# An RWKV attention and two-MLP kernel on one core: the second group's k products in split operands, and later preparation for the last five units

## The chip, the cores and the metric

The kernel runs on one core of a Trainium2 chip. The metric is the device time of one execution in microseconds; the number given for a kernel is the median of several runs. TensorE is called PE here, VectorE DVE, ScalarE ACT, GpSimd POOL and SyncE SP, as in the profile; SP and ACT also issue DMAs.

## What is computed

Three layers in float32, over 2 batches of 768 tokens.

```python
# attention: 8 heads of 48; state is 48 x 48 per head
for t in range(S):
    cur = einsum('bhd,bhe->bhde', u[None] * kt, vt)
    y[:, :, t] = einsum('bhd,bhde->bhe', rt, state + cur)
    state = wt[:, :, :, None] * state + einsum('bhd,bhe->bhde', kt, vt)
# first MLP, x is the attention's output, 384 wide
xk = mu_k * x + (1.0 - mu_k) * x_prev        # x_prev: the token before
xr = mu_r * x + (1.0 - mu_r) * x_prev
k = np.maximum(xk @ w_k, 0.0)                # 384 -> 1024
x = 1 / (1 + exp(-(xr @ w_r))) * (k * k @ w_v)
# second MLP, with a mixing over tokens
h = gelu(x @ w_in); u, v = halves of h
out = x + (u * (w_sg @ norm(v) + b_sg)) @ w_out
```

## The kernel before

Tokens are worked in four groups of 384 (0 to 3). In a group attention has four **units**, one per pair of heads, so units 0 to 15; unit i belongs to group i // 4. A unit is chunked in three parts of 128 tokens. Its work on PE is four steps: S(i) (`attn_sc`: transposes of kp, the sums `ab` of the direct term, and the scores `sc`), K(i) (`attn_kv`: the state products `kv`), Y(i) (`attn_y`: the masked scores `am` times v), Z(i) (`attn_z`: the carried states, then the output `yo`, which a DMA puts into the group's x, `xx`).

Before S(i), `attn_prep` makes on DVE the decay scans `pf` and `pr`, and the operands `kp`, `rp` and `ru`. `scans` runs it up to the two scans and issues the next unit's loads; `products` runs the rest; `prep` runs all. After S(i), DVE takes `ru<-ab` and the two mask products `am` (L482); after K(i) it makes the states `zt` and `zcar` (L508, L510), which ACT scales into `sblk` and `scar` (L524) for Z.

The first MLP of a group has three stages on PE: eight k steps (`moe1_k`, three 128-row products each over the blocks of x), three r steps (`moe1_r`), and v steps (`moe1_v`, 24 products of each output block). The matmul helper is `mm` (L595, matmuls at L603). While a group's MLP runs, the next group's units are put between its steps: the list `plan` at the start of `emit` says after which k, r and v step which S, K, Y and Z comes, with estimated durations from which `TS` and `TE` (times of start and end) are made. PE follows that list by hand. On the other engines a scheduler orders the instructions by the priority that `at(t)` gives them; `tc.issue_after(x)` keeps an instruction from being placed before x on its engine. Each engine then works its queue strictly in order, and waits at its head.

Products have two forms. **Natural**: both operands float32, one matmul instruction per product, which the trace shows as two records. **Split**: each operand is a rounded high part and the rest, and a product is three matmuls (high x high, high x low, low x high). For split products ACT makes the high part by a copy and the low part is a subtraction (`split_to`, L311): of the weights on POOL, of x on DVE (L642, L643). `NAT` says how many groups use the natural form of k, r and v: groups 0 and 1 for k, group 0 for r and v.

`moe1_prep(s, which)` makes the operand of group s, k (0) or r (1), block by block: ACT scales x by mu (`dx`, L637), DVE adds the scaled token before (L639), and if split, ACT copies the high part and DVE subtracts. Block 2 of group 1 needs unit 7's output. `split1` splits a weight of the first MLP; its low part goes to the next free tile of a ring of 21 that the full weights use too. In group 1, a k step's `split1` made one low part of k on POOL. The r and v weights are split at the end of group 0's v stage (L711). `load64` loads and converts a weight (`top` on ACT, then L309 on DVE); the w_in weights of the second MLP (`wf`) take tiles of the same ring.

Of the kernel before, what the change touches and what calls it, by code (L numbers as in the profile page):

```python
# [24 lines left out]
NP = H // 2  # L25
# [19 lines left out]
B_AM = 2  # L45
B_KP = 3
T_START = 7
T_GAP = 2.5
T_TAIL = 9.0
VQ = 4  # L50
# [4 lines left out]
L_CK = 6  # L55
L_PREP = 5
L_UN = 14
NAT = {"k":2,"r":1,"v":1}
SUB0 = (3,)
NVN = 8  # L60
RA = 12
# [8 lines left out]
def emit(tc, tin, nin, vt, consts, ucp, pars, b_sg, w_k, w_v, w_r, w_in, w_sgT, w_out, outT):  # L70
# [239 lines left out]

    def split_to(hi, lo, full, dl, e):  # L311
        with at(dl):
            A.activation(hi, full, AF.Copy)  # L313
            e.tensor_tensor(lo, full, hi.bitcast(F32), ALU.subtract)  # L314

    def full1(nm, i, shape):
        wt[nm, i] = (pl["w"].tile(shape, F32, name="w" + nm, tag="wl", bufs=NW1 + SPARE),)

    def split1(nm, i, dl):
        if not split_ops[0]:  # L320
            return
        full = wt[nm, i][0]
        shape = list(full.shape)
        lo = pl["w"].tile(shape, F32R, name="w" + nm + "l", tag="wl", bufs=NW1 + SPARE)
        if early["hi"] % 2 == 0:
            early["t"] = pair()
        o = early["hi"] % 2 * WT
        early["hi"] += 1
        hi = early["t"][:, o:o + WT].rearrange("p (c f) -> p c f", c=shape[1])
        split_to(hi, lo, full, dl, PL)  # L330
        wt[nm, i] = (hi, lo)

    def conv_moe1(first=0, last=2 * KF + KM):
        def one(nm, i, src, dl):
# [141 lines left out]
    def self_am(i, am, sc, tY):  # L476
        s = st[i]
        nc_ = subs[i // NP][2]
        for h in range(2):
            with at((TS["K", i] - 1.4 if i >= NP else tY - 1.2) + 0.4 * h):  # L480
                mask = cmask[:, None, :].to_broadcast([128, nc_, CH])
                V.tensor_tensor(am[:, h], sc[h], mask, ALU.mult)  # L482
        s["at"] = am

    def attn_kv(i):
        tY = TS["Y", i] if i < NP else TS["K", i] + 1.1
        s = st[i]
        hp = i % NP
        g, c0, nc_ = subs[i // NP]
        si = i // NP  # L490
        last = g % GB == GB - 1 and c0 + nc_ == CG
        nk = nc_ - 1 if last else nc_
        kv = pq.tile([128, 512], F32, name="kv", tag="kv", bufs=1)
        kv3 = kv[0:PR, 0:nc_ * D].rearrange("p (c d) -> p c d", d=D)
        for c in range(nk):
            for h in range(2):
                hs = slice(h * HP, HP if h == 0 else PR)
                PE.matmul(kv3[hs, c], s["kt"][:, c, hs], uv[i][:, c, h * D:h * D + D], start=(c == 0), stop=(c == nk - 1),  # L498
                          skip_group_check=True)
        zt = pa.tile([PR, max(1, nc_), D], F32, name="zt", tag="zt", bufs=2)  # L500
        first = g % GB == 0 and c0 == 0
        us = [None if first else scar[hp]]
        z = None if first else (zcar[:, (si + 1) % 2, hp, 0:D], zcar[:, (si + 1) % 2, hp, D:D + 1])
        for c in range(nk):
            o = zcar[:, si % 2, hp, 0:D] if c == nc_ - 1 else zt[:, c]
            with at(tY - 0.6 + (3 if c == nc_ - 1 else 0.2 * c)):
                if z is None:
                    V.tensor_copy(o, kv3[:, c])  # L508
                else:
                    V.scalar_tensor_tensor(o, z[0], z[1], kv3[:, c], ALU.mult, ALU.add)  # L510
            z = (o, s["pe"][c])
            sb = scar[hp] if c == nc_ - 1 else sblk[i % 2][c]

            def scaled(c=c, o=o, sb=sb):
                if c == nc_ - 1:
                    with at(tY + 3):
                        A.activation(zcar[:, si % 2, hp, D:D + 1], s["pe"][c], AF.Copy)
                with at(tY - 0.5 + (3 if c == nc_ - 1 else 0.2 * c)):
                    for h in range(2):
                        hs = slice(h * HP, h * HP + D)  # L520
                        if i == NP - 1 and c < nc_ - 1:
                            V.tensor_scalar(sb[hs, hs], o[hs], s["pe"][c][hs], None, ALU.mult)
                        else:
                            A.activation(sb[hs, hs], o[hs], AF.Copy, scale=s["pe"][c][hs])  # L524

            if i < NP:
                s.setdefault("late" if c == nc_ - 1 else "soon", []).append(scaled)
            else:
                scaled()
            us.append(sb)  # L530
        s["us"] = us
# [131 lines left out]
    def moe1_k(s, f):  # L663
        nat, nt = is_nat(s, "k"), subs[s][2] * CH
        ps = mm_tile()[:, 0:nt]
        mm(ps, [(part(wt["k", f], slice(None), j), part(m1[s, 0], slice(None), j)) for j in range(KM)])
        kr = pl["w"].tile([128, nt], F32, name="kr", tag="kr", bufs=2)
        te, tv = TE["k", s, f], TS["v", s, 0] + f * MM[s, "v"]
        with at(te):
            m1[s, "ev", f] = A.activation(kr, ps, AF.Relu).ins  # L670
        vn = is_nat(s, "v") and (f < NVN or not split_ops[0])
        kh = pl["w"].tile([128, nt], F32 if vn else F32R, name="kh", tag="kh", bufs=KF)
        dl = min(te + 1, tv - 2)
        if s == NAT["k"] - 1:
            split1("k", f, TS["k", s + 1, f])
        if vn:
            with at(dl):
                A.activation(kh, kr, AF.Square)
            m1[s, "k", f] = (kh,)
            return  # L680
        if f % 2 == 0:
            m1[s, "kl"] = klpair(F32R)
        kl = m1[s, "kl"][:, f % 2 * WT:f % 2 * WT + nt]
        with at(dl):
            A.activation(kh, kr, AF.Square)
            A.activation(kr, kr, AF.Square)  # L686
            V.tensor_tensor(kl, kr, kh.bitcast(F32), ALU.subtract)  # L687
        m1[s, "k", f] = (kh, kl)
# [10 lines left out]
    def moe1_v(s, j, q):  # L699
# [9 lines left out]
        with at(TE["v", s, j] - 0.5):  # L709
            V.tensor_tensor(x2[g][:, j, c0 * CH:(c0 + n) * CH], ps, m1[s, "r", j], ALU.mult)  # L710
        if s == NAT["r"] - 1 and j == KM - 1 and split_ops[0]:  # L711
            with tc.issue_after(st[2 * NP - 2]["ev"]):
                for f in range(KM):
                    split1("r", f, TS["r", s + 1, f])
                for f in range(NVN):
                    split1("v", f, TS["v", s + 1, 0] + f * 0.49)
# [223 lines left out]
                pass  # L940

    def scans(i):
        if i >= 1:
            load_unit(i + 1)
        head["prep", i] = attn_prep(i)
        next(head["prep", i])
        next(head["prep", i])

    def products(i):
        for _ in head["prep", i]:  # L950
            pass
# [14 lines left out]
    for n, key in enumerate(keys[:n_in]):  # L966
# [38 lines left out]
        if kd == "S" and g == NP:  # L1005
            prep(NP + 1)
            conv_moe1(3)
        if kd == "Z" and g >= NP:
            prep(g + 2)
            if g % NP == NP - 1:  # L1010
                moe1_prep(g // NP, 0)
        if kd == "k" and key[2] == (0 if g in (0, NS - 1) else KM - 1):
            moe1_prep(g, 1, [] if g in (0, NS - 1) else [m1[g, "ev", f] for f in range(KM)])
        if key == ("r", 0, 0):
            with at(TS["S", 2 * NP] - 20):
# [89 lines left out]
```

## Time and profile before

| | us |
|---|---|
| median of 3 runs (348.79 to 349.15) | 349.04 |
| the profiled execution | 351.7 |
| its span, first to last instruction | 349.8 |
| PE busy in it | 337.5 |
| DVE, ACT, POOL busy in it | 237.6, 180.9, 40.8 |
| mean granted PE clock, share of full speed | 0.994 |

Stages in the span: attention of group 0 until about 31, group 0's MLP with units 4 to 7 until 87.6, group 1's MLP with units 8 to 11 until 142.7, groups 2 and 3 until about 217, then the second MLP. A row gives start and duration in us; "x12" counts records; in brackets stands how long the engine was idle before the row and what released it. Matmuls overlap, so the spacing of starts tells what one costs, and its own duration does not. For the other engines too the spacing of starts is a little shorter than the duration of one.

### The profile page before, as it was taken

The numbers are of one execution on the slowest core, as the hardware profiler recorded it, in microseconds if no ns is written. First come the engines' busy times: TensorE is split into PE (matmuls) and PEld (weight loads), VectorE is DVE, ScalarE is ACT, GpSimd is POOL, SyncE is SP. The second block draws the span as 40 slices with busy tenths as digits, with TensorE's granted clock in tenths as the row PEclk, the third lists the DMA queues.
The fourth block names the chain that finished last, engine by engine and source line by source line (L and its number), as shares of the span: only waits on it lengthen the run. The fifth ranks groups of instructions, "written<-read, shape, count | busy, mean of one in ns | idle before, by whom it ended". The sixth has DMA issues, their size and how long they took to land.

```text
span 349.8 us, 5957 instructions
## 1 busy us (share of the span) xinstructions
PE 337.5 (96%) x2155; PEld 287.6 (82%) x2155; DVE 237.6 (68%) x520; ACT 180.9 (52%) x427; POOL 40.8 (12%) x64
## 2 busy tenths in 40 slices
PE   7999999999979989999999999999999999999993
PEld 3776677666546769988899999899899999999993
DVE  6987999794468886496438753298789951645531
ACT  3465986475665652686428894668171316211100
POOL 3000000064622000000004044000000000000000
PEclk9999999999989999999999999999999999999999
DMA  8787963762304541001113232822322010100022
GB/s 227 196 301 233 321 166 90 200 162 56 133 18 103 143 133 36 4 16 42 37 27 132 80 105 69 254 53 62 79 63 57 0 46 24 44 25 0 0 72 75
DMA packets 23750, 33.97 MB, mean 97 GB/s; under 512 B 3504, under 2 KB 18032, under 8 KB 23712
## 3 DMA queue, kind: packets, MB, share of 16 engines
q1 hardware_dynamic: 21568, 31.09, 30.7%
q10 hardware_dynamic: 2144, 2.41, 2.4%
q8 instruction: 19, 0.31, 0.4%
q14 instruction: 19, 0.16, 0.1%
HBM read 28.77 MB, written 2.36 MB: 89 GB/s over the span
## 4 chain that ended last, share of the span: by engine, by line
PE 64%; ACT 4%; DVE 4%; DMA 2%; issue 1%; SPq 1%; ACTq 0%; DVEq 0%
PE mm L603 31%; PE mn L603 27%; PE y L542 2%; DMA stg<-w_in 1%; PE sc L459 1%; PE y L556 1%; ACT wh L313 1%; PE ab L455 1%; ACT sblk L524 1%; DVE dx L639 1%; DMA xx<-yo 1%; DVE kl L687 1%; PE kv L498 1%; ACT dx L637 0%; ACT kr L670 0%
## 5 line engine op out<-in xcount | busy, mean ns | idle before, releaser
L603 PE MATMUL mm<-xkh,wk 128*128 128x384 f32 x96 | 35.6, 515 | 0.0
L591 ACT ACTIVATE gah<-gt 128x384 fp32r<-128x384 f32 x16 | 8.4, 526 | 43.3 <-DVE gt L783 43.3
L603 PEld LDWEIGHTS mm<-xkh,wk 128*128 128x128 f32 x96 | 18.2, 198 | 12.9 <-issue 2.3
L637 ACT ACTIVATE dx<-xx,par 128x384 f32<-128x384 f32 x22 | 13.3, 610 | 26.9 <-DMA xx<-yo 25.8
L524 ACT ACTIVATE sblk<-zt,pf 48x48 f32<-48x48 f32 x60 | 19.8, 331 | 11.0 <-DVE zt L508 7.1
L603 PE MATMUL mm<-kh,wh 128*128 128x384 f32 x64 | 22.1, 345 | 0.0
L603 PE MATMUL mm<-kh,wvl 128*128 128x384 f32 x64 | 21.6, 338 | 0.0
L603 PE MATMUL mm<-kl,wh 128*128 128x384 f32 x64 | 21.6, 337 | 0.0
L687 DVE TENSOR_TENSOR kl<-kr,kh 128x384 fp32r<-128x384 f32 x24 | 14.3, 594 | 10.5 <-ACT kr L686 10.5
L314 POOL TENSOR_TENSOR w2l<-wf,w2h 128x384 fp32r<-128x384 f32 x12 | 12.9, 1090 | 62.9 <-ACT w2h L313 62.9
L603 PE MATMUL mn<-wsh,vh 128*128 128x384 f32 x60 | 20.0, 334 | 0.0
L603 PE MATMUL mn<-wsl,vh 128*128 128x384 f32 x60 | 20.0, 334 | 0.0
L603 PE MATMUL mn<-wsh,vl 128*128 128x384 f32 x60 | 20.0, 334 | 0.0
L414 DVE TENSOR_TENSOR_SCAN pf<-uw,d1f 112x387 f32<-112x387 f32 x16 | 15.3, 959 | 4.8 <-DMA uw<-tin 2.2
L639 DVE SCALAR_TENSOR_TENSOR dx<-xx,par,dx 128x384 f32<-128x384 f32 x15 | 12.1, 809 | 9.6 <-ACT dx L637 9.6
L670 ACT ACTIVATE kr<-mm 128x384 f32<-128x384 f32 x27 | 12.9, 478 | 10.8 <-PE mm L603 8.9
L542 PE MATMUL y<-am,uv 128*48 128x128 f32 (+1 forms) x192 | 15.3, 278 | 2.4 <-DVE am L482 2.4
L482 DVE TENSOR_TENSOR am<-sc,cst 128x384 f32<-128x384 f32 x32 | 16.1, 545 | 1.1 <-PE sc L459 1.1
L603 PE MATMUL mm<-kh,wv 128*128 128x384 f32 x48 | 16.3, 490 | 0.0
L459 PEld LDWEIGHTS sc<-rp,kp 48*128 48x128 f32 x192 | 12.0, 187 | 5.1 <-issue 4.5
L419 DVE TENSOR_TENSOR_SCAN pr<-uw,d1r 112x387 f32<-112x387 f32 x16 | 15.4, 962 | 0.4
L459 PE MATMUL sc<-rp,kp 48*128 48x128 f32 x192 | 15.0, 289 | 0.0
(215 smaller groups left out, 965.3 us busy)
## 6 DMA issues: line engine op xcount, KB each, us to landing
urk<-tin SPq DMA_DIRECT2D x26, 144.0 KB, 3.5
wh<-w_k SPq DMA_DIRECT2D x8, 384.0 KB, 3.8
stg<-w_in SPq DMA_DIRECT2D x8, 384.0 KB, 3.6
wq<-tin SPq DMA_DIRECT2D x16, 168.0 KB, 2.4
wsf<-w_sgT SPq DMA_DIRECT2D x12, 192.0 KB, 4.0
outT<-ot SPq DMA_DIRECT2D x12, 192.0 KB, 1.9
uv<-nin ACTq DMA_DIRECT2D x14, 144.0 KB, 2.9
uw<-tin SPq DMA_DIRECT2D x26, 72.8 KB, 3.3
```

What stands on the lines that cost most here:

```text
L314: e.tensor_tensor(lo, full, hi.bitcast(F32), ALU.subtract)
L414: V.tensor_tensor_scan(pf[:, 0:n1], w[:, 0:n1], d1f[:, 0:n1], 1.0, ALU.mult, ALU.max)
L419: V.tensor_tensor_scan(pr[:, 1:wl][:, ::-1], w[:, 1:wl][:, ::-1], dr[:, 1:wl][:, ::-1], 0.0, ALU.mult, ALU.add)
L459: PE.matmul(sc[h][:, c], s["kp"][hs, c], s["rp"][hs, c], start=True, stop=True)
L482: V.tensor_tensor(am[:, h], sc[h], mask, ALU.mult)
L524: A.activation(sb[hs, hs], o[hs], AF.Copy, scale=s["pe"][c][hs])
L542: PE.matmul(y3[hs, c], uv[i][:, c, h * D:PW if h else HP], s["at"][:, h, c], start=(c == 0), stop=False, skip_group_check=True)
L603: PE.matmul(ps, l, r, start=(first and k == 0), stop=(last and k == len(prods) - 1))
L637: A.activation(d, xj[:, 1 + t0:1 + t1], AF.Copy, scale=mu[:, j:j + 1])
L639: V.scalar_tensor_tensor(ops[0][:, j] if nat else d, xj[:, t0:t1], nu[:, j:j + 1], d, ALU.mult, ALU.add)
L670: m1[s, "ev", f] = A.activation(kr, ps, AF.Relu).ins
L687: V.tensor_tensor(kl, kr, kh.bitcast(F32), ALU.subtract)
```

## The change

- `NAT["k"]` goes from 2 to 1: group 1's k steps use split operands too, so 24 natural products become 72 split matmuls, and blocks of group 1's x for k get a high and a low part.
- The eight k weights are split at the end of group 0's v stage, right after unit 7's output eviction in the order, ACT for the high part and DVE (was POOL) for the low part. The r and v weights follow behind the last k copy on ACT; before they followed unit 6's eviction.
- Group 1's r operand is prepared right behind its k operand (`moe1_prep(1, 1)` after Z(7)), not spread over the first k steps.
- Units 11 to 15: the scans are held behind the states of the unit two before, and kp, rp, ru behind the mask products of the unit just before. Before they were placed by priority alone.

```diff
@@ -45,6 +45,7 @@
 B_AM = 2
 B_KP = 3
 T_START = 7
+UPIN = 11
 T_GAP = 2.5
 T_TAIL = 9.0
 VQ = 4
@@ -55,7 +56,7 @@
 L_CK = 6
 L_PREP = 5
 L_UN = 14
-NAT = {"k":2,"r":1,"v":1}
+NAT = {"k":1,"r":1,"v":1}
 SUB0 = (3,)
 NVN = 8
 RA = 12
@@ -310,13 +311,14 @@
 
     def split_to(hi, lo, full, dl, e):
         with at(dl):
-            A.activation(hi, full, AF.Copy)
+            i = A.activation(hi, full, AF.Copy).ins
             e.tensor_tensor(lo, full, hi.bitcast(F32), ALU.subtract)
+        return i
 
     def full1(nm, i, shape):
         wt[nm, i] = (pl["w"].tile(shape, F32, name="w" + nm, tag="wl", bufs=NW1 + SPARE),)
 
-    def split1(nm, i, dl):
+    def split1(nm, i, dl, e=PL):
         if not split_ops[0]:
             return
         full = wt[nm, i][0]
@@ -327,8 +329,9 @@
         o = early["hi"] % 2 * WT
         early["hi"] += 1
         hi = early["t"][:, o:o + WT].rearrange("p (c f) -> p c f", c=shape[1])
-        split_to(hi, lo, full, dl, PL)
+        ins = split_to(hi, lo, full, dl, e)
         wt[nm, i] = (hi, lo)
+        return ins
 
     def conv_moe1(first=0, last=2 * KF + KM):
         def one(nm, i, src, dl):
@@ -479,7 +482,7 @@
         for h in range(2):
             with at((TS["K", i] - 1.4 if i >= NP else tY - 1.2) + 0.4 * h):
                 mask = cmask[:, None, :].to_broadcast([128, nc_, CH])
-                V.tensor_tensor(am[:, h], sc[h], mask, ALU.mult)
+                s["am"] = V.tensor_tensor(am[:, h], sc[h], mask, ALU.mult).ins
         s["at"] = am
 
     def attn_kv(i):
@@ -505,9 +508,9 @@
             o = zcar[:, si % 2, hp, 0:D] if c == nc_ - 1 else zt[:, c]
             with at(tY - 0.6 + (3 if c == nc_ - 1 else 0.2 * c)):
                 if z is None:
-                    V.tensor_copy(o, kv3[:, c])
+                    s["zt"] = V.tensor_copy(o, kv3[:, c]).ins
                 else:
-                    V.scalar_tensor_tensor(o, z[0], z[1], kv3[:, c], ALU.mult, ALU.add)
+                    s["zt"] = V.scalar_tensor_tensor(o, z[0], z[1], kv3[:, c], ALU.mult, ALU.add).ins
             z = (o, s["pe"][c])
             sb = scar[hp] if c == nc_ - 1 else sblk[i % 2][c]
 
@@ -671,8 +674,6 @@
         vn = is_nat(s, "v") and (f < NVN or not split_ops[0])
         kh = pl["w"].tile([128, nt], F32 if vn else F32R, name="kh", tag="kh", bufs=KF)
         dl = min(te + 1, tv - 2)
-        if s == NAT["k"] - 1:
-            split1("k", f, TS["k", s + 1, f])
         if vn:
             with at(dl):
                 A.activation(kh, kr, AF.Square)
@@ -709,7 +710,10 @@
         with at(TE["v", s, j] - 0.5):
             V.tensor_tensor(x2[g][:, j, c0 * CH:(c0 + n) * CH], ps, m1[s, "r", j], ALU.mult)
         if s == NAT["r"] - 1 and j == KM - 1 and split_ops[0]:
-            with tc.issue_after(st[2 * NP - 2]["ev"]):
+            with tc.issue_after(st[2 * NP - 1]["ev"]):
+                for f in range(KF):
+                    hi = split1("k", f, TS["k", s + 1, f], V)
+            with tc.issue_after(hi):
                 for f in range(KM):
                     split1("r", f, TS["r", s + 1, f])
                 for f in range(NVN):
@@ -940,7 +944,7 @@
                 pass
 
     def scans(i):
-        if i >= 1:
+        if i >= 1 and i + 1 < NU:
             load_unit(i + 1)
         head["prep", i] = attn_prep(i)
         next(head["prep", i])
@@ -1005,11 +1009,20 @@
         if kd == "S" and g == NP:
             prep(NP + 1)
             conv_moe1(3)
+        if kd == "S" and g >= UPIN - 1 and g + 1 < NU:
+            with tc.issue_after(st[g]["am"]):
+                products(g + 1)
+        if kd == "Z" and g >= NP and g + 2 < UPIN:
+            prep(g + 2)
+        elif kd == "Z" and g >= NP and g + 2 < NU:
+            with tc.issue_after(st[g]["zt"]):
+                scans(g + 2)
         if kd == "Z" and g >= NP:
-            prep(g + 2)
             if g % NP == NP - 1:
                 moe1_prep(g // NP, 0)
-        if kd == "k" and key[2] == (0 if g in (0, NS - 1) else KM - 1):
+                if g // NP == 1:
+                    moe1_prep(g // NP, 1)
+        if kd == "k" and key[2] == (0 if g in (0, NS - 1) else KM - 1) and g != 1:
             moe1_prep(g, 1, [] if g in (0, NS - 1) else [m1[g, "ev", f] for f in range(KM)])
         if key == ("r", 0, 0):
             with at(TS["S", 2 * NP] - 20):
```

ACT's queue where group 0's v stage ends (`yo` is unit 7's output, `wh<-wk` the high parts of the k weights, `dx` the scaling of x). Before:

```order
L313 ACTIVATE wh<-wv 128x384 x2
L517 ACTIVATE zcar<-pf 112x1
L313 ACTIVATE wh<-wk 128x384 x8
L568 ACTIVATE yo<-y 112x384
L637 ACTIVATE dx<-xx_78,par 128x384
```

And now:

```order
L520 ACTIVATE zcar<-pf 112x1
L571 ACTIVATE yo<-y 112x384
L314 ACTIVATE wh<-wk 128x384 x8
L314 ACTIVATE wh<-wr 128x384
L640 ACTIVATE dx<-xx_78,par 128x384 x2
L314 ACTIVATE wh<-wr 128x384 x2
L645 ACTIVATE xkh<-dx 128x384
L645 ACTIVATE xrh<-dx 128x384
L314 ACTIVATE wh<-wv 128x384
```

The output of unit 7 stands ahead of the k copies now, and r's and most of v's copies come behind them, between the parts of the x operands.

DVE's queue from there to unit 8's mask products (`xx_77<-mm` are evictions of group 0's v stage, `wkl` the low parts of the k weights, `xkl` and `xrl` those of x, `kl` those of the squared k, `wf` a w_in weight). Before:

```order
L710 TENSOR_TENSOR xx_77<-mm,rs 128x384
L639 SCALAR_TENSOR_TENSOR xkh<-xx_78,par_76,dx 128x384
L710 TENSOR_TENSOR xx_77<-mm,rs 128x384
L639 SCALAR_TENSOR_TENSOR dx<-xx_78,par_76,dx 128x384
L687 TENSOR_TENSOR kl<-kr,kh 128x384
L643 TENSOR_TENSOR xrl<-dx,xrh 128x384
L462 TENSOR_TENSOR ru<-ab,uvt 112x384
L639 SCALAR_TENSOR_TENSOR dx<-xx_78,par_76,dx 128x384
L687 TENSOR_TENSOR kl<-kr,kh 128x384
L482 TENSOR_TENSOR am<-sc,cst 128x384 x2
```

And now, from the second four of the eight `wkl`:

```order
L315 TENSOR_TENSOR wkl<-wk,wh 128x384 x4
L642 SCALAR_TENSOR_TENSOR dx<-xx_78,par_76,dx 128x384 x2
L646 TENSOR_TENSOR xkl<-dx,xkh 128x384
L646 TENSOR_TENSOR xrl<-dx,xrh 128x384
L642 SCALAR_TENSOR_TENSOR dx<-xx_78,par_76,dx 128x384
L711 TENSOR_TENSOR xx_77<-mm,rs 128x384
L642 SCALAR_TENSOR_TENSOR dx<-xx_78,par_76,dx 128x384
L646 TENSOR_TENSOR xrl<-dx,xrh 128x384 x2
L688 TENSOR_TENSOR kl<-kr,kh 128x384
L465 TENSOR_TENSOR ru<-ab,uvt 112x384
L485 TENSOR_TENSOR am<-sc,cst 128x384
L688 TENSOR_TENSOR kl<-kr,kh 128x384
```

The k weights' low parts stand in DVE's queue now, ahead of the last block of the k operand, and all of the r operand comes ahead of unit 8's mask products; the second mask product follows the second `kl`.

DVE's queue from the mask products of unit 10 to its first states. Before:

```order
L482 TENSOR_TENSOR am<-sc,cst 128x384 x2
L428 SCALAR_TENSOR_TENSOR ru<-urk_110,cst 112x384
L419 SCALAR_TENSOR_TENSOR pr<-uw_105,d1r 112x387
L309 SCALAR_TENSOR_TENSOR wf<-stg,top_127 128x384
L639 SCALAR_TENSOR_TENSOR dx<-xx_79,par_76,dx 128x384
L423 TENSOR_TENSOR kp<-urk_108,pr 112x384
L687 TENSOR_TENSOR kl<-kr,kh 128x384
L508 COPY zt<-kv 112x48
```

And now:

```order
L485 TENSOR_TENSOR am<-sc,cst 128x384 x2
L426 TENSOR_TENSOR kp<-urk_110,pr 112x384
L429 TENSOR_TENSOR rp<-urk_110,pf 112x384
L431 SCALAR_TENSOR_TENSOR ru<-urk_110,cst 112x384
L511 COPY zt<-kv 112x48
L642 SCALAR_TENSOR_TENSOR dx<-xx_79,par_76,dx 128x384
L513 SCALAR_TENSOR_TENSOR zt<-zt,pf,kv 112x48
```

Unit 12's scan and kp no longer stand there, and unit 11's kp, rp and ru come right behind unit 10's masks. On PE, Z(10) and S(11) stood between r steps 1 and 2 and now stand behind step 2; the order of the v steps after them is nearly the same.

## Rows read from the trace of the kernel before

**Rows 1.** The page: busy time, share of the span and instructions of each engine

```profile
PE 337.5 (96%) x2155; PEld 287.6 (82%) x2155; DVE 237.6 (68%) x520; ACT 180.9 (52%) x427; POOL 40.8 (12%) x64
```

**Rows 2.** Busy us by stretch (instructions) of each engine, granted clock, DMA share, GB/s

```profile
core 0: us, PE busy (x) PEld busy (x) DVE busy (x) ACT busy (x) POOL busy (x), PEclk, DMA share, GB/s
95.50:99.80 4.30, 1.85 (x25) 1.22 (x24) 3.69 (x7) 2.62 (x7) 0.99 (x1) 0.98 0.14 36
99.80:106.00 6.20, 6.20 (x19) 3.79 (x19) 3.48 (x7) 4.88 (x14) 1.29 (x2) 0.74 0.11 26
117.50:128.30 10.80, 9.27 (x74) 7.52 (x73) 9.21 (x21) 5.98 (x15) 0.00 (x0) 1.00 0.57 161
128.30:142.70 14.40, 14.40 (x102) 13.98 (x101) 9.89 (x20) 4.55 (x11) 0.19 (x1) 1.00 0.21 55
142.70:170.00 27.30, 27.30 (x215) 23.61 (x214) 19.56 (x41) 20.21 (x48) 0.00 (x0) 1.00 0.12 29
```

**Rows 3.** PE's timeline, 87 to 126 us: start, us, instruction, [wait before it]

```profile
87.63 4.03 PE L603 MATMUL mm<-xkh,wk 128*128 128x384 f32 x12
91.50 0.45 PE L437 MATMUL kt_ps<-cst,kp 112*128 112x112 f32 x3
...
93.40 2.20 PE L603 MATMUL mm<-xkh,wk 128*128 128x384 f32 x6
...
98.51 1.38 PE L542 MATMUL y<-am,uv 128*64 128x128 f32 x12 [2.42 <-DVE am L482]
99.82 5.72 PE L603 MATMUL mm<-xkh,wk 128*128 128x384 f32 x12
105.38 0.60 PE L556 MATMUL y<-rp,sblk 112*112 112x128 f32 x4
105.82 0.45 PE L437 MATMUL kt_ps<-cst,kp 112*128 112x112 f32 x3
...
123.74 0.47 PE L556 MATMUL y<-rp,sblk 112*112 112x128 f32 x2 [1.30 <-ACT sblk L524]
...
124.75 0.45 PE L437 MATMUL kt_ps<-cst,kp 112*128 112x112 f32 x3
```

**Rows 4.** PE's timeline, 142 to 146 us, first and last of 18 split matmuls

```profile
142.74 0.34 PE L603 MATMUL mm<-xkh,wh 128*128 128x384 f32 x1
...
145.70 0.34 PE L603 MATMUL mm<-xkh,wkl 128*128 128x384 f32 x1
```

**Rows 5.** PE's timeline, 79 to 80 us

```profile
79.45 0.60 PE L556 MATMUL y<-rp,sblk 112*112 112x128 f32 x4
```

**Rows 6.** ACT's timeline, 79 to 87 us

```profile
79.57 3.40 ACT L313 ACTIVATE wh<-wk 128x384 fp32r<-128x384 f32 x8
82.88 0.46 ACT L568 ACTIVATE yo<-y 112x384 f32<-112x384 f32 x1
86.26 0.62 ACT L637 ACTIVATE dx<-xx,par 128x384 f32<-128x384 f32 x1 [2.92 <-DMA xx<-yo]
```

**Rows 7.** VectorE's timeline, 107 to 123 us

```profile
107.49 0.55 DVE L687 TENSOR_TENSOR kl<-kr,kh 128x384 fp32r<-128x384 f32 x1
107.96 0.54 DVE L566 TENSOR_TENSOR yo<-y,ru 112x384 f32<-112x384 f32 x1
...
122.78 0.20 DVE L508 COPY zt<-kv 112x48 f32<-112x48 f32 x1
```

**Rows 8.** GpSimd's (POOL) and VectorE's timeline, 71 to 77 us

```profile
71.07 3.51 POOL L314 TENSOR_TENSOR wrl<-wr,wh 128x384 fp32r<-128x384 f32 x3 [33.73 <-ACT wh L313]
...
73.64 1.36 DVE L426 TENSOR_TENSOR rp<-urk,pf 112x384 f32<-112x384 f32 x1
...
74.54 2.58 POOL L314 TENSOR_TENSOR wvl<-wv,wh 128x384 fp32r<-128x384 f32 x2
74.92 1.35 DVE L428 SCALAR_TENSOR_TENSOR ru<-urk,cst 112x384 f32<-112x384 f32 x1
```

**Rows 9.** Line 314 on GpSimd: ns min/median/max, first and last start

```profile
L314 POOL TENSOR_TENSOR wvl<-wv,wh x8: 987/998/1315, 74.5 to 88.6; 128x384 fp32r<-128x384 f32 x8
```

## Prediction

> **What bounds the kernel now.** I read the busy shares first, then stretches of some ten us, then PE's waits in the worst stretch, then the queues of the engines that release them. PE is busy 96% of the span [rows 1]: what ends last is nearly always PE's own order, so an edit pays if it shortens PE's work or one of its waits. The stretches show where waits are [rows 2]: PE works 1.85 of 4.30 us from 95.5, and 9.27 of 10.80 from 117.5. Both lie in the second group (group 1, units 8 to 11 in between), which starts with its first k product at 87.63. From 128.3 to 170 no us is idle. PE's timeline names three losses in group 1 [rows 3]. Y(8) waits 2.42 us for the mask product am(8). Behind it the clock is at 0.74 on average in the stretch from 99.8 [rows 2], so part of it ran at 1.2 instead of 2.4 GHz: six products take 99.82 to 105.38, 5.56 us, where six took 87.63 to 91.50, 3.87; the drop costs 1.7. Z(10) waits 1.30 for scaled states, and from 123.74 takes 1.01 to the next transposes where Z(8) took 105.38 to 105.82, 0.44: 1.9 us lost there in all.
>
> **Term 1, split k products.** A k product of group 1 in float32 takes 3.87 / 6 = 0.645 us [rows 3]. Split matmuls start 0.174 apart (142.74 to 145.70 is 17 spacings), so a product of three takes 0.522 [rows 4]. 24 products times 0.123 is **2.9 us**, all on PE's path. The Trainium skill (FP8 and Floating Point Precision, TensorE Precision Notes) has true FP32 as four passes through the array; against three split passes that frees one pass of 384 columns, 0.16 us at 2.4 GHz, so 3.8 us by that rule and 344.0 in the end. No row here shows single passes, and 0.123 is what the rows give.
>
> **Term 2, what makes the split operands, and Y(8).** The eight k splits leave GpSimd and come before k0. The eviction of unit 7's output, yo(7), now stands ahead of the eight copies on ACT: Z(7) ends at 80.05 [rows 5], so yo(7) can end near 80.55 instead of 83.34, and the copies follow 0.425 apart, 80.5 to 83.9 [rows 6]. VectorE's instructions follow each other 0.47 apart [rows 7]; eight subtractions and one v eviction from 81.0 end near 85.25. The splits are thus hidden behind the v products that keep PE busy until 87.63. The last block of the k operand needs yo(7)'s transfer (2.92 from the eviction's end to the scaling [rows 6], so 83.5) and ACT after nine copies, 84.3.
>
> From there it gets tight. GpSimd's eleven r and v splits, which ran mostly before 87 and met little, start at 85.2, when k's sixth slot and the first r copy are free, and VectorE has ten instructions with two SBUF operands to do before am(8) is finished. The rows show what that costs [rows 8]: two such VectorE instructions that meet back-to-back GpSimd splits end 1.27 us apart (75.00 and 76.27), not 0.47, with each split at 1.0 [rows 9]. Walking VectorE's new order with 1.27 where GpSimd has a split ready and 0.47 elsewhere (ACT supplies the v copies between other work, some 0.5 each): third block of xkl at 89.2, which k0 wants at 88.85 (0.35 wait); xrl 90.4, 93.1, 94.3; kl(0) 95.6; ru(8) 96.1; first half of am(8) 96.6; kl(1) 97.4; second half **97.9**. On ACT the same queue brings kt(8) at 95.1. PE: k0 and k1 until 91.1, S(8) with its 1.90 [rows 3] until 93.0, k2 until 94.7, 0.45 wait for kt(8), then 2.3 for am(8). Sum of waits 3.1 against 2.42: **minus 0.7**. Y(8) starts at 97.9 instead of 98.51. Its bounds: no meeting at all gives am(8) at 95.2 and waits of 0.6 (plus 1.8); every one of the ten at 1.27 and the other four at 0.47 gives 85.2 + 14.6 = 99.8 (minus 2.6). I take the walk, since it uses the price of the nearest rows where GpSimd has work.
>
> **Term 3, the clock.** A wait of 2.42 was followed by the drop, and about the same wait remains, so I keep the drop: 0. If it stays away, plus 1.7.
>
> **Term 4, Z(10).** Before, the first state copy zt(10) ran at 122.78 [rows 7], behind a kl, unit 12's scan and kp, a weight conversion and a scaling on VectorE; Z(10) came right after r1. Now kp, rp, ru of unit 11 alone stand between am(10) and zt(10), the weight conversions have moved ahead, and PE runs r1 and r2 (18 matmuls, 3.1 us) between Y(10) and Z(10). ACT's scaling for unit 10 gets some 2 us of room, although a dx that waits for unit 9's transfer now stands in front of it. The **1.9** of Z(10) go.
>
> **What costs nothing.** Two k blocks more to split on ACT and VectorE before Z(7), 2 x 0.5 each: GpSimd no longer holds VectorE there, which repays them; without that cover they delay unit 10's scans, and S(10) comes 30 us later. Preparation held behind states and masks: kp(11) follows am(10) at once, and PE has K(10), Y(10), r1, r2 and Z(10), over 4 us, before S(11); units 12 to 15 have a whole unit's distance. If am(10) were late by more than that, S(11) would wait for kp(11). On SP unit 14's decay load moves behind two w_in loads that wait for VectorE's conversions; it is needed some 25 us later. The first w_in conversion on VectorE must wait for GpSimd's tenth split (its tile takes that slot), and the second state of unit 8 queues behind it: 99.3 for the split, 101.7 for the scaled state, and Z(8) comes at 102.5 without and 104.1 with the clock drop. That is 0.8 us of cover at worst.
>
> Sum: 2.9 - 0.7 + 0 + 1.9 = 4.1 us. After 128.3 PE had no wait until 170 [rows 2], and the next group's operand hangs on Z(11), which keeps its place among the v products, so the gain is passed on. The profiled execution took 351.7 (span 349.8, 1.9 around it), 2.7 above the median 349.04; a difference inside the span is carried to the median: **344.9**.
>
> **Rivals.** (a) VectorE and GpSimd don't meet: ACT delivers the v copies so late that GpSimd is empty when VectorE needs the port. For it: several v copies stand behind kr on ACT. Against: r's three and v's first are ready at once. Terms 2 and 3 become +1.8 and +1.7: gain 8.3, **340.7**.
> (b) Slower: VectorE falls behind through am(9). Every meeting costs 1.27, am(8) is done at 99.8, 1.9 after the forecast, and the conversions behind GpSimd's tenth and eleventh split, with kl(4), push am(9) behind K(9), which the walk makes just in time. A second wait like Y(8)'s costs 2.4 and the drop 1.7: 6.0 together, **350.9**. It decides once the new waits pass 4.1. Against: by then GpSimd is done. The Trainium skill (SBUF — State Buffer, Who interferes with whom) calls the shared port an exclusive lock that the second instruction waits for in full; by that rule eleven splits could hold VectorE for eleven us, which speaks for (b). The pair above shows 0.8 per meeting, so the trace agrees with the lock but not with eleven full turns.
> (c) The gain is handed back: ACT, into whose queue eleven r and v copies move here, gets late with kr and kt in group 1, or group 2's operand comes late. PE's waits return, 2 to 4 us: **348**.
>
> **How the numbers follow.** A measurement here can tell about 0.2%, 0.7 us, from no change. Forecast, 343.2 to 346.6: 0.50. (a), 340 to 343.2: 0.20. (c) in part, 346.6 to 348.3: 0.12, in full, within 0.7 of before: 0.07. (b): 0.11. So faster 0.82, same 0.07, slower 0.11. The range 340.8 to 348.4 holds the forecast, most of (a) and the partial (c), about 0.78; it takes in the gain of term 2's better bound with the clock, and of its worse bound without it.
>
> **What would show it.** Right: 24 split products from about 87.6 at 0.52 each; Y(8)'s wait for am still 1.5 to 3 us, VectorE instructions of 1.2 to 1.4 from 85 to 97 beside GpSimd's rows; Z(10) with no wait; v's first product near 124 instead of 128.3. Wrong: Y(8) without a wait and full clock (a), waits at Y(9) or Z(8) (b), or waits of PE after 128 (c). If the k products took more than 0.6 each, term 1 is wrong.

## The result, and the profile after

The changed kernel takes **346.38 us** (median of 19 runs, 346.0 to 348.44), the kernel before 349.65 (19 runs beside it, 348.5 to 354.35); the ratio is **0.9897, interval 0.9875 to 0.9919**, some 3.3 to 3.6 us faster. The profiled execution took 346.58 with a span of 344.8, against 351.7 and 349.8 before; before's runs lie in two clumps (ten at 348.5 to 349.7, nine from 351.0 up) and its profiled one in the upper, so the spans' difference of 5.0 overstates the change.

The page after, engine line, and the stretches of [rows 2] (columns as there):

```profile
PE 332.2 (96%) x2179; PEld 289.9 (84%) x2179; DVE 243.7 (71%) x531; ACT 182.6 (53%) x430; POOL 32.9 (10%) x56
```

```profile
core 0: us, PE busy (x) PEld busy (x) DVE busy (x) ACT busy (x) POOL busy (x), PEclk, DMA share, GB/s
95.50:99.80 4.30, 2.38 (x28) 1.97 (x29) 3.02 (x7) 4.26 (x11) 3.67 (x5) 1.00 0.13 34
99.80:106.00 6.20, 6.20 (x45) 5.52 (x44) 3.51 (x7) 4.75 (x14) 0.74 (x1) 1.00 0.31 90
117.50:128.30 10.80, 10.80 (x92) 9.53 (x88) 9.87 (x22) 6.10 (x16) 0.00 (x0) 1.00 0.44 116
128.30:142.70 14.40, 14.40 (x91) 13.81 (x91) 6.26 (x12) 4.92 (x13) 0.19 (x1) 1.00 0.08 22
142.70:170.00 27.30, 27.30 (x221) 23.75 (x220) 22.88 (x50) 18.79 (x45) 0.00 (x0) 1.00 0.13 32
```

From 117.5 to 170 PE is never idle (before: 9.27 of 10.80 in the first of these stretches), and no stretch has a lowered clock (before: 0.74 from 99.8). From 95.5 it still works only 2.38 of 4.30. PE's timeline, with what answers to [rows 3]:

```profile
87.61 0.63 PE L606 MATMUL mm<-xkh,wh 128*128 128x384 f32 x1
88.08 0.34 PE L606 MATMUL mm<-xkl,wh 128*128 128x384 f32 x1
...
89.50 0.45 PE L606 MATMUL mm<-xkl,wh 128*128 128x384 f32 x1 [0.21 <-DVE xkl L646]
...
91.52 0.45 PE L440 MATMUL kt_ps<-cst,kp 112*128 112x112 f32 x3
...
96.68 0.52 PE L501 MATMUL kv<-uv,kt 128*64 128x48 f32 x12 [1.43 <-ACT kr L687]
...
98.26 0.86 PE L545 MATMUL y<-am,uv 128*48 128x128 f32 x10 [0.73 <-DVE am L485]
99.05 0.44 PE L606 MATMUL mm<-xkh,wh 128*128 128x384 f32 x1
...
102.29 0.60 PE L559 MATMUL y<-rp,sblk 112*112 112x128 f32 x4
...
106.71 0.52 PE L501 MATMUL kv<-uv,kt 128*64 128x48 f32 x12 [0.25 <-ACT top L308]
108.12 1.32 PE L545 MATMUL y<-am,uv 128*64 128x128 f32 x12 [0.90 <-DVE am L485]
109.37 0.44 PE L606 MATMUL mm<-xkh,wh 128*128 128x384 f32 x1
...
121.16 0.60 PE L559 MATMUL y<-rp,sblk 112*112 112x128 f32 x4
...
123.49 0.44 PE L606 MATMUL mm<-kh,wh 128*128 128x384 f32 x1
```

The first v product starts at 123.49, right behind S(11), instead of at 128.32, where r step 2 stood between. Unit 8 waits 1.43 + 0.73 where it waited 2.42, Z(10) not at all, and unit 9 has new waits, 0.25 and 0.90. Before, unit 9 had none:

```profile
109.84 0.55 PE L498 MATMUL kv<-uv,kt 128*64 128x48 f32 x12
110.23 1.05 PE L542 MATMUL y<-am,uv 128*64 128x128 f32 x12
111.21 2.20 PE L603 MATMUL mm<-xkh,wk 128*128 128x384 f32 x6
```

VectorE's and GpSimd's timelines there, against [rows 7] and [rows 8]:

```profile
85.52 2.62 DVE L642 SCALAR_TENSOR_TENSOR dx<-xx,par,dx 128x384 f32<-128x384 f32 x2
88.07 1.38 DVE L646 TENSOR_TENSOR xkl<-dx,xkh 128x384 fp32r<-128x384 f32 x1
...
94.76 1.35 DVE L688 TENSOR_TENSOR kl<-kr,kh 128x384 fp32r<-128x384 f32 x1
96.04 0.55 DVE L465 TENSOR_TENSOR ru<-ab,uvt 112x384 f32<-112x384 f32 x1
...
97.66 0.55 DVE L485 TENSOR_TENSOR am<-sc,cst 128x384 f32<-128x384 f32 x1
...
99.60 1.36 DVE L310 SCALAR_TENSOR_TENSOR wf<-stg,top 128x384 uint32<-128x384 uint32 x1 [1.27 <-POOL wvl L315]
...
104.64 0.56 DVE L310 SCALAR_TENSOR_TENSOR wf<-stg,top 128x384 uint32<-128x384 uint32 x1 [1.66 <-ACT top L308]
...
106.06 0.55 DVE L465 TENSOR_TENSOR ru<-ab,uvt 112x384 f32<-112x384 f32 x1
```

```profile
85.31 3.72 POOL L315 TENSOR_TENSOR wrl<-wr,wh 128x384 fp32r<-128x384 f32 x3 [47.69 <-DVE wkl L315]
...
91.93 3.77 POOL L315 TENSOR_TENSOR wvl<-wv,wh 128x384 fp32r<-128x384 f32 x3 [1.61 <-ACT wh L314]
```

VectorE's instructions with two SBUF operands took 1.3 a piece where GpSimd had a split to do, as forecast; `ru` ends at 96.59 and the second `am` at 98.2. Two w_in conversions (`wf`) stood 1.27 and 1.66 us at the head of its queue. Unit 8's second state came behind the first of them, and ACT waited for it:

```profile
101.16 0.68 ACT L527 ACTIVATE sblk<-zt,pf 48x48 f32<-48x48 f32 x2 [1.35 <-DVE zt L513]
```

The name behind K(8)'s wait is wrong. ACT's kt(8) ended at 95.37 (94.93 + 0.44), long before. But `ab`, the direct term's sums, and `kv` are tiles of one PSUM tag with one buffer, so K(8) must wait for VectorE's `ru<-ab`. K(8) starts at 96.68, 0.09 after that read. At all nine waits of a K in this trace and those of the runs below, 0.09 to 0.11 lie between the two, whatever the profile named (ACT kr, kh, dx, top, zcar or "issue"). So both waits at unit 8, and both at unit 9, were VectorE's queue.

### The profile page after: what moved, and what is told of

The parts are those of the page before. It is cut to its first block, busy times and chain, and to the rows that moved or that the text cites. A ratio compares the mean times of both kernels' runs of the same rounds, so it can differ in the third digit from the quotient of the medians.

```text
span 344.8 us, 5996 instructions
## 1 busy us (share of the span) xinstructions
PE 332.2 (96%) x2179; PEld 289.9 (84%) x2179; DVE 243.7 (71%) x531; ACT 182.6 (53%) x430; POOL 32.9 (10%) x56
## 4 chain that ended last, share of the span: by engine, by line
PE 85%; DVE 5%; ACT 4%; DMA 3%; issue 1%; POOL 0%; SPq 0%; DVEq 0%; ACTq 0%; POOLq 0%
PE mm L606 41%; PE mn L606 27%; PE sc L462 4%; PE y L545 3%; PE y L559 3%; ACT wh L314 2%; DMA wh<-w_r 2%; PE kv L501 2%; PE y L548 1%; PE kt_ps L440 1%; PE ab L458 1%; DMA uw<-tin 1%; PE mm L937 1%; PE kt_ps L445 1%; DVE dx L642 1%
## 5 line engine op out<-in xcount | busy, mean ns | idle before, releaser
L606 PE MATMUL mm<-xkh,wh 128*128 128x384 f32 x57 | 20.3, 357 | 0.0
L688 DVE TENSOR_TENSOR kl<-kr,kh 128x384 fp32r<-128x384 f32 x24 | 15.3, 636 | 6.1 <-ACT kr L687 6.1
L606 PE MATMUL mm<-xkl,wh 128*128 128x384 f32 x57 | 19.3, 338 | 0.2 <-DVE xkl L646 0.2
L606 PE MATMUL mm<-xkh,wkl 128*128 128x384 f32 x57 | 19.2, 337 | 0.0
L606 PE MATMUL mm<-xkh,wk 128*128 128x384 f32 x48 | 17.0, 497 | 0.0
L642 DVE SCALAR_TENSOR_TENSOR dx<-xx,par,dx 128x384 f32<-128x384 f32 x18 | 13.8, 776 | 3.0 <-ACT dx L640 3.0
```

The source lines that it names most:

```text
L606: PE.matmul(ps, l, r, start=(first and k == 0), stop=(last and k == len(prods) - 1))
L642: V.scalar_tensor_tensor(ops[0][:, j] if nat else d, xj[:, t0:t1], nu[:, j:j + 1], d, ALU.mult, ALU.add)
```

## The experiments

My theory at first: PE's shorter products and Z(10)'s place are the gain, the rest of the change is cover. The first of four runs kept the split products alone, and three took one thing out each.

**Split products alone**: no hold, r operand spread as before.

```diff
-UPIN = 11
+UPIN = 16
...
-                if g // NP == 1:
-                    moe1_prep(g // NP, 1)
-        if kd == "k" and key[2] == (0 if g in (0, NS - 1) else KM - 1) and g != 1:
+        if kd == "k" and key[2] == (0 if g in (0, NS - 1) else KM - 1):
```

> The split k products alone: the preparation of units 11 to 15 placed by priority as before, and the second group's r operand spread over its k steps as before. My theory: what pays is PE's own work, 24 products at 0.52 instead of 0.645 us (2.9), and the new place of Z(10) behind r2 on PE, which comes with the shorter k steps and not with the hold (1.9); without the r operand ahead of unit 8's masks Y(8) should wait about 1 us less than the changed kernel's 0.73 + 1.43. So it is as fast as the changed kernel's 346.4 or faster: 345.3 to 346.6, Z(10) with no wait. Rival: the hold is what lets zt(10) come in time; then Z(10) or S(11) waits 1 to 2 us again and the time is 347.5 to 348.5.

350.43 us, ratio 1.0009 (0.9978 to 1.0039): no gain at all. Both readings missed it: Z(10) did not wait, and K(8) waited 4.44 us, with a clock drop behind it. The profiled execution, 351.74, also had a drop from 39.6 to 43.1 and began the k steps 1.7 us late (89.28), so some of its own time has another cause.

**All but the split products**: `NAT["k"]` back to 2, the k weights split in `moe1_k` on GpSimd as before.

```diff
-NAT = {"k":1,"r":1,"v":1}
+NAT = {"k":2,"r":1,"v":1}
...
+        if s == NAT["k"] - 1:
+            split1("k", f, TS["k", s + 1, f])
...
-                for f in range(KF):
-                    hi = split1("k", f, TS["k", s + 1, f], V)
-            with tc.issue_after(hi):
```

> Everything but the split k products: the second group's k products stay in float32, the k weights are split on GpSimd within the k steps, and the hold and the early r operand are kept. My theory: the 2.9 us of the products are lost, Z(10) goes back between r1 and r2 on PE, where the hold shortens its wait of 1.3 to some 0.3; 347.8 to 349. Products 0.64 apart. Rival: the reordering is the gain and the split products are given back elsewhere; then it is 346 to 347, with waits at Y(8) and Y(9) as short as in the changed kernel.

349.88, ratio 0.9985 (0.9949 to 1.0021), somewhat slower than expected. Its profile has the float32 products behind Y(8) at full clock, six in 3.97 us (100.04 to Z(8)):

```profile
100.04 4.14 PE L606 MATMUL mm<-xkh,wk 128*128 128x384 f32 x12
104.01 0.60 PE L559 MATMUL y<-rp,sblk 112*112 112x128 f32 x4
```

The changed kernel's six split ones took 3.24 (99.05 to 102.29). Added up over the eight k steps at full clock, start to start and without waits, float32 takes 15.98 here and split 13.46 in the run with late splits below: the products are worth **2.5 us**.

**No hold** on units 11 to 15 (`UPIN = 16` alone).

> The changed kernel without the hold on units 11 to 15. My theory: the hold is worth little, since PE has r1 and r2 between Y(10) and Z(10): 346.0 to 346.8, no wait at Z(10) over 0.3 us. Rival: preparation gets in front of unit 8's and 9's masks or of zt(10) on VectorE again; Y(9) waits 1 to 2 us more than its 0.9, or Z(10) 1 us, and the time is 347.3 to 348.5.

348.67, ratio 0.9953 (0.9925 to 0.9981): close to the rival's time. Y(10) waited 0.67: unit 12's two scans, which the hold keeps back, stood in front of unit 10's masks on VectorE (113.24 and 114.45). The same waits at unit 8 (1.43 + 0.74) were followed by a clock drop here, which the changed kernel's profile lacks:

```profile
95.50:99.80 4.30, 2.59 (x26) 1.99 (x26) 3.03 (x7) 4.07 (x11) 3.68 (x4) 0.83 0.15 34
99.80:106.00 6.20, 6.20 (x40) 5.52 (x39) 5.06 (x10) 4.95 (x14) 0.52 (x1) 0.85 0.33 92
```

The drop explains little of the lost 2 us. Z(8) comes 1.35 later than in the changed kernel (103.64 against 102.29), but S(10) only 0.37 (113.43 against 113.06), since unit 9's waits shrink from 1.15 to 0.18: PE would have waited there anyway. And two of the twelve runs, at a mean clock of 0.998, took 348.54 and 348.94 like the others.

**R operand spread** over the k steps as before, hold kept (the second half of the first diff).

> The changed kernel with the second group's r operand spread over its k steps as before. My theory: the r operand's subtractions on VectorE, at 1.3 us beside GpSimd, stand in front of unit 8's masks, so without them Y(8)'s two waits of 1.43 + 0.73 shrink by 0.7 to 1.5, unless ACT's queue with kt(8) at 94.93 sets them, which moves little; Y(9) keeps about 1 us. 345.2 to 346.2. Rival: ACT's queue alone sets Y(8), and the r parts then collide with unit 9: 346.4 to 347.5, Y(9) waiting over 1.5.

348.86, ratio 0.9967 (0.9934 to 0.9999): both missed. VectorE's and PE's timelines:

```profile
87.79 0.56 DVE L711 TENSOR_TENSOR xx<-mm,rs 128x384 f32<-128x384 f32 x1
95.50 1.33 DVE L310 SCALAR_TENSOR_TENSOR wf<-stg,top 128x384 uint32<-128x384 uint32 x1 [7.16 <-POOL wvl L315]
...
98.22 0.55 DVE L465 TENSOR_TENSOR ru<-ab,uvt 112x384 f32<-112x384 f32 x1
98.69 1.01 DVE L485 TENSOR_TENSOR am<-sc,cst 128x384 f32<-128x384 f32 x2
```

```profile
98.87 0.52 PE L501 MATMUL kv<-uv,kt 128*64 128x48 f32 x12 [4.43 <-ACT dx L640]
```

Without the r parts in front of it, the scheduler put a w_in conversion ahead of unit 8's masks. It waited 7.16 us for GpSimd's tenth weight split, whose tile of the ring it takes, with `ru`, K(8) and `am` behind it. In the split-alone run the wait at K(8) is the same to 0.01.

So a second theory: **the w_in conversion's place in VectorE's queue decides whether the split products pay**, and GpSimd's splits beside VectorE's x operands set what is left. The next four runs hold the conversions back, and one the splits as well.

**Conversions late** (line 310 held behind unit 11's states):

```diff
+    hold = {"wf": contextlib.nullcontext}
...
-        with at(dl - lc):
+        with at(dl - lc), hold["wf"]():
...
+        hold["wf"] = lambda: tc.issue_after(st[11]["zt"]) if split_ops[0] else contextlib.nullcontext()
```

> The changed kernel with the w_in conversions on VectorE (wf) held behind the states of unit 11, so that none stands in VectorE's queue among the work of units 8 and 9. My theory: the waits of K(9) and Y(9), 0.25 and 0.90 in the changed kernel, come from two conversions that wait at the head of VectorE's queue; they go, and Y(8) keeps its 1.43 + 0.73: 344.9 to 345.6. Rival: the waits at unit 9 come from ACT and the kl before the masks, or the moved conversions delay the evictions in the v stage; then 346.0 to 347.

346.41, ratio 0.9889 (0.9849 to 0.993): the waits at unit 9 went, the time stayed. Its profile has the unchanged waits at unit 8 with a clock drop behind them: six products took 3.96 instead of 3.24, and PE started the k steps 0.58 later. `ru` of unit 9 ended at 106.37, 0.24 earlier than in the changed kernel, although PE came to Z(8) 1.95 later (104.24); so the conversions did hold it up, but with PE that late the profile cannot tell what the two waits alone cost. The drop is seen in one execution; in the other five the mean clock is 0.989 or 0.99, lower than in that one (0.994), so it is likely there too.

**Conversions and weight splits late**: r's and v's eleven splits held on ACT behind unit 8's `kt` (`ktc` is the instruction that copies it).

```diff
-            with tc.issue_after(hi):
-                for f in range(KM):
-                    split1("r", f, TS["r", s + 1, f])
-                for f in range(NVN):
-                    split1("v", f, TS["v", s + 1, 0] + f * 0.49)
...
+        if kd == "S" and g == 2 * NP:
+            with tc.issue_after(st[g]["ktc"]):
+                for f in range(KM):
+                    split1("r", f, TS["r", 1, f])
+                for f in range(NVN):
+                    split1("v", f, TS["v", 1, 0] + f * 0.49)
```

> As the run before, and the eleven r and v weight splits held on ACT behind unit 8's kt, so that GpSimd does not work while VectorE prepares the x operands and unit 8's masks. My theory: VectorE's instructions from 85 to 97 us then end 0.5 apart instead of 1.3, and the wait at k0 (0.21) and those at K(8) and Y(8) (1.43 + 0.73) shrink to under 0.7 together: 343.2 to 344.0. Rival 1: the meeting of the two engines does not set these waits; the same time as the run before. Rival 2: the splits now run from 95 to 107 us beside unit 9's preparation and bring back a wait of 1 to 2 us at Y(9) or r0: 344.5 to 345.5.

**342.72**, ratio **0.9787** (0.9747 to 0.9828), the fastest of all, 6.9 us below before and 3.7 below the change. VectorE's timeline, then PE's:

```profile
85.75 0.61 DVE L644 SCALAR_TENSOR_TENSOR dx<-xx,par,dx 128x384 f32<-128x384 f32 x1
86.28 0.55 DVE L648 TENSOR_TENSOR xkl<-dx,xkh 128x384 fp32r<-128x384 f32 x1
...
91.96 0.55 DVE L467 TENSOR_TENSOR ru<-ab,uvt 112x384 f32<-112x384 f32 x1
...
94.43 1.01 DVE L487 TENSOR_TENSOR am<-sc,cst 128x384 f32<-128x384 f32 x2
```

```profile
94.39 0.55 PE L503 MATMUL kv<-uv,kt 128*64 128x48 f32 x12
...
96.28 0.44 PE L608 MATMUL mm<-xkh,wh 128*128 128x384 f32 x1
```

The same `dx` and `xkl` take 0.61 and 0.55 where they took 1.3 and 1.38; `ru` ends 4.1 us earlier, and K(8) starts with no wait. GpSimd's first split starts at 93.08 now.

**R operand spread, conversions late** (the fourth run with the hold of the conversions).

> The run without the early r operand again, with the w_in conversions held behind the states of unit 11. My theory: the 4.43 us wait at K(8) there was the w_in conversion that had moved ahead of unit 8's masks and stood 7.16 us at the head of VectorE's queue for GpSimd's last split; held back, K(8) and Y(8) wait 0.5 to 2 us together and the time is 344.5 to 345.8, so that the early r operand itself is worth nothing, only where the conversion stands. Rival: r's x blocks on ACT and VectorE themselves hold kt(8) and the masks; K(8) still waits over 3 us: 347.5 to 349.

344.36, ratio 0.984 (0.9798 to 0.9882): as expected, 4.5 below the fourth run by this edit alone, and K(8) starts at 94.56 with no wait. The conversion is shown to be what stood there. GpSimd's and VectorE's timelines show what the meeting slows:

```profile
88.86 9.08 POOL L316 TENSOR_TENSOR wvl<-wv,wh 128x384 fp32r<-128x384 f32 x8
```

```profile
93.43 0.55 DVE L466 TENSOR_TENSOR ru<-ab,uvt 112x384 f32<-112x384 f32 x1
93.90 1.01 DVE L486 TENSOR_TENSOR am<-sc,cst 128x384 f32<-128x384 f32 x2
...
95.70 1.37 DVE L647 TENSOR_TENSOR xrl<-dx,xrh 128x384 fp32r<-128x384 f32 x1
```

`ru` and both `am`, which read one operand from PSUM, kept their 0.5 us beside eight splits in a row, while `xrl`, with both operands in SBUF, took 1.37.

**Split products alone, conversions late** (the first run with the same hold).

> The split products alone again (no hold on units 11 to 15, r operand spread as before), with the w_in conversions held behind the states of unit 11. My theory: it was the conversion at the head of VectorE's queue that ate the split products' gain; without it 345.0 to 346.3, Z(10) and S(11) with no wait over 0.7. Rival: the hold of units 11 to 15 is needed too; masks or states come late behind scans and kp, Y(10) or Z(10) waits 1 to 2 us: 347 to 348.5.

346.13, ratio 0.9892 (0.9858 to 0.9927), 4.3 below the first run: the theory's time. So split products and this one hold of the conversions give the whole gain of the change, without its hold of units 11 to 15 and its early r operand. Z(8) waits 0.64 and unit 9 0.69 + 0.90, with no conversion near, and its profile has a drop near 107.

Three runs and a second look at before closed it.

**Weight splits late alone**, conversions as in the change.

> The changed kernel with the eleven r and v weight splits held on ACT behind unit 8's kt, and the w_in conversions left as they are. In the order they then stand behind unit 9's masks on VectorE, and the first of them waits for GpSimd's tenth split. My theory: GpSimd's work beside the x operands is the main cost by itself; the tenth split ends near 105, when unit 9's masks end, so the conversion waits little: 342.5 to 343.6. Rival: the conversion stands 1 to 2 us at the head of VectorE's queue in front of unit 9's states and Z(9) waits: 344 to 345.5, so both edits are needed.

344.14, ratio 0.9828 (0.9792 to 0.9864): 2.2 below the change, 1.4 above both edits; the rival's time, though the wait came at Y(10) (0.84) and not at Z(9). Two conversions stand in front of unit 9's first state, which starts at 107.29 instead of 104.65 with both edits. Both edits seem needed: the two ratios' intervals overlap, the runs themselves (343.81 to 344.88 against 342.64 to 342.98) do not.

**Both edits, r operand spread.**

> Both edits (w_in conversions behind unit 11's states, r and v splits behind unit 8's kt), and the r operand spread over the k steps as before. My theory: with GpSimd quiet until 93 the place of the r operand is worth nothing: within 0.6 of 342.72, 342.4 to 343.4. Rival: r's blocks now meet the late splits from 93 to 106 and push unit 9's masks: Y(9) waits 1 to 2 us, 343.8 to 345.

344.57 (343.44 to 345.92), ratio 0.9829 (0.9791 to 0.9868): slower than expected and the rival's time, with 0.68 at Y(9). Its profiled execution, the slowest, began the k steps at 89.98, 2.7 late, with a clock drop from 40 to 44. At a mean clock of 0.996 or more, where such a drop is unlikely, it took 343.44 to 343.95; how much is the r operand's own place stays open, at most 1.9.

**Both edits, no hold.**

> Both edits, and no hold on units 11 to 15. Without the hold the changed kernel took 2.3 us more, with a clock drop near 99 us in its profile, and the split products alone with the late conversions 1.8 more, with one near 107. My theory: the hold is worth at most 0.5 us by itself and the rest was the clock; with no wait left at unit 8 there is no drop, and this is 342.6 to 343.6. Rival: the hold keeps scans and kp out of the way of masks and states at units 9 to 11, whatever the clock does: waits of 1 us and more at Y(9), Y(10) or Z(10), 344.2 to 345.5.

346.71, ratio 0.9901 (0.9865 to 0.9936): the rival is right, the hold is worth 4.0 here. VectorE, then PE:

```profile
99.68 1.76 DVE L418 TENSOR_TENSOR_SCAN pf<-uw,d1f 112x387 f32<-112x387 f32 x1
...
101.69 1.37 DVE L423 TENSOR_TENSOR_SCAN pr<-uw,d1r 112x387 f32<-112x387 f32 x1
...
104.21 0.54 DVE L467 TENSOR_TENSOR ru<-ab,uvt 112x384 f32<-112x384 f32 x1
```

```profile
104.86 0.52 PE L503 MATMUL kv<-uv,kt 128*64 128x48 f32 x12 [1.08 <-issue]
106.55 1.80 PE L547 MATMUL y<-am,uv 128*64 128x128 f32 x12 [1.18 <-DVE am L487]
```

Unit 11's scans, stretched to 1.76 and 1.37 beside GpSimd, stand in front of `ru`; K(9) starts 0.11 after it (so "issue" is again the PSUM tile). A drop follows. One run with a mean clock of 0.999 took 346.66 like the others, so how the 4.0 divide between waits and clock is not settled.

**The kernel before again.**

> The kernel before, unchanged, for a second profile. Two thirds of its runs took 348.8 to 350.5 us at a mean clock of 0.995 or more, the profiled one 351.7 at 0.994. My theory: the difference is the clock drop behind Y(8). If this profile has none, Y(8) still waits about 2.4 us and Z(10) 1.3, six float32 k products behind Y(8) take 3.9 to 4.0 us instead of 5.56, and the span is 346.9 to 347.6. Rival: the faster runs lack the wait at Y(8) itself, not the drop alone.

352.0, with the same wait and drop:

```profile
98.42 1.32 PE L542 MATMUL y<-am,uv 128*64 128x128 f32 x12 [2.40 <-DVE am L482]
```

```profile
99.80:106.00 6.20, 6.20 (x19) 3.74 (x20) 3.49 (x7) 4.87 (x13) 1.36 (x2) 0.74 0.09 26
```

So what the faster half of its runs lacks was not seen. The clocks speak for the drop: of the 62 executions of this kernel beside the experiments 20 took 351 us or more, 19 of them at a mean clock of 0.994 or less, and 41 of the 42 faster ones had 0.995 or more. But the medians of the two lots lie 2.7 apart, more than the price of the drop below, so it may not be all.

## Why the prediction was right

Faster, as forecast at 0.82, and 346.38 lies in the range, 1.5 above the 344.9. By its steps:

- **Term 1, 2.9.** Measured 2.5, so it was sized 0.4 too high. The spacing of 0.174 was right, but the first split matmul behind other work takes 0.47 (87.61 to 88.08) or 0.28 (99.05 to 99.33), and eight steps pay that several times. The estimate from the Trainium skill's count of passes (FP8 and Floating Point Precision, TensorE Precision Notes) was 3.8; the trace does not bear it out.
- **Term 2, minus 0.7.** Measured plus 0.2: waits of 0.21 + 1.43 + 0.73 against 2.42, and K(8) and Y(8) themselves 0.2 shorter. The walk put `xkl` at 89.2 (89.45), `ru` at 96.1 (96.6), the second `am` at 97.9 (98.2). Its price of 1.27 for a meeting held, and the run with late splits shows that the meeting caused the waits. One step of it was wrong and cost nothing: K(8) did not wait for kt(8) on ACT but for `ru`.
- **The shared port.** The rows show 0.8 added per instruction with two SBUF operands (1.36 against 0.56 for `xrl`) and nothing for those with one in PSUM. Eleven full turns, the reading that spoke for rival (b), did not come. The Trainium skill (SBUF — State Buffer, Who interferes with whom) calls the port an exclusive lock; the trace agrees with that for one instruction at a time.
- **Term 3, 0.** The wait behind which the clock fell stayed, and the changed kernel's profile shows no drop, while the profiles without hold and with late conversions do, at the same waits. The drop costs the six products of before 1.6 (5.56 against 3.97), not 1.7. Next to nothing of it is in Y(8): its 1.31 stands against 1.25 at full clock for the changed kernel's Y(9) (108.12 to 109.37), the same twelve records behind a wait. And a drop need not cost the changed kernel anything: its four runs at a mean clock of 0.989 to 0.991 took 346.26 to 346.45, those at 0.994 and more 346.0 to 346.58, and the three at 0.985 and 0.986 took 348.05 to 348.44.
- **Term 4, 1.9.** Right: Z(10) waits for nothing, and 1.30 + 0.57 are gone. The split-alone run shows that PE's order with r1 and r2 in front does it, not the hold.
- **"0.8 us of cover at worst."** This step failed. It followed the first conversion to Z(8), which had cover; nobody followed it and the second one (1.66 for ACT's `top`) to `ru(9)` and `am(9)`. The trace has the path: ACT stood 1.35 for the state behind the first conversion, and its `kr` for the next `kl` on VectorE, in front of `ru(9)`, ended at 104.91 (104.42 + 0.49). They cost unit 9 0.25 + 0.90 by this reading, and K(9) and Y(9) themselves took 0.4 more behind the waits (106.71 to 109.37 less 0.90 is 1.76; before, 109.84 to 111.21 is 1.37). It is the place that rival (b) named; two late instructions there, not a queue late all through.
- **"What costs nothing", the hold and the early r operand.** Also failed. I costed the hold at nothing, and the early r operand only as part of VectorE's load in term 2, never as what keeps a conversion from moving up. By the ratios the change without the hold loses 2.0 us, without the early r operand 2.4, without the split products 3.1, more together than the whole gain of 3.6. They do not add up; as far as the traces show, each keeps VectorE's queue from the same few waits.

Summed: 2.5 + 0.2 + 1.9 - 1.15 - 0.4 is 3.05 us, near the 3.3 of the medians; the spans' 5.0 have in addition the drop's 1.6 that both profiles of before show and the changed kernel's does not, and 0.35 stay unassigned. That the forecast's 4.1 came so near is in part luck: term 2 came out 0.9 better than forecast, and unit 9, which stood at nothing, took 1.55. Rival (c), a gain handed back, fell for the stages behind 128: no wait there. It came true in small inside group 1.

## What to carry to other kernels

Before you move work off one queue, ask which instruction of that queue will come forward, and what it waits for: here a conversion for a much later stage moved up behind the removed work and ate the gain of 24 faster products. Hold such early work back explicitly; one such hold here was worth 4.3 and 4.5 us where the change's order had not kept the conversion back, and nothing in the median where it had (346.41 against 346.38). Where two engines work on operands in the same memory, keep the helper's batch away from the stretch in which the other makes what PE waits for.

## What the runs showed of the hardware that was not expected

- A GpSimd subtraction does not slow every VectorE instruction: 1.36 against 0.56 us with two SBUF operands, 0.55 and 0.5 unchanged with one in PSUM. The forecast had counted on it (ten instructions at 1.27, four at 0.47); the runs show it.
- The two scans of unit 11 took 1.76 and 1.37 us beside GpSimd's late splits (both edits, no hold) and 0.96 each where GpSimd was idle (the change, no hold, 102.77 and 103.98).
- Waits of 1.43 and 0.73 were followed by a fall to 1.2 GHz in the profiles of two kernels (granted clock 0.83 to 0.85 in the stretches from 95.5 and 99.8) and by none in that of a third (1.00 in both). Here the drop could not be forecast from the waits alone.
- A drop that lies in front of another wait is partly absorbed by it: 1.35 us at Z(8) were 0.37 at S(10) in the run without the hold.
- A releaser named by the profile can be a bystander: nine waits named ACT or "issue", and all ended 0.09 to 0.11 us behind a VectorE read of the PSUM tile that both share by the code.
